# Sorted rows in groups of four and one stream scatter for two blocks, in a mixture-of-experts kernel

## The chip, the cores and the metric

One core of one Trainium2 chip runs the whole program. The metric is the device time of one execution in microseconds (us), median of several executions. The engines are named as in the profile: PE (TensorE, matmuls; PEld is its weight load), ACT (ScalarE), DVE (VectorE), POOL (GpSimd) and SP (SyncE, which only issues transfers here).

## What is computed

A causal 7-tap convolution over 8 sequences of 3584 rows, 192 wide, with one softmaxed set of taps for each of 8 heads of 24 columns. Its 28,672 result rows go through a top-1 mixture of 8 experts. Cut to what matters:

```python
logits = x @ w_gate                          # (28672, 8)
e_idx = np.argmax(logits, axis=1)            # one expert for each row
gate_w = softmax(logits)[row, e_idx]
eom = sigmoid(x @ w_output_gate)
for e in range(8):
    mask = e_idx == e
    h = np.maximum(x[mask] @ w1[e], 0.0)     # 192 -> 1024
    ye = h @ w2[e]                           # 1024 -> 192
    out[mask] = gate_w[mask, None] * eom[mask, e, None] * ye
```

The inputs are one fixed draw, so which row goes to which expert is fixed too.

## The kernel before

The 28,672 rows are cut into 16 units of 1792 rows, and a unit into 8 blocks of 224 rows (two half blocks of 112 rows, `l = 0, 1`, are sorted together). Three kinds of work share the engines.

**Front.** `front_a(u)` does the convolution on PE (tile `cv`), transposes it (`tt`) and computes both gates (`gb`). `front_b(u)` picks each row's expert, computes its place in its block (`pos`) and the places of the block's groups in the stream (`dst`, `du`), and then sorts block by block: `prep(i)` builds 0/1 matrices `pm` on DVE, four matmuls with 128 columns of weights (line 541) put the block's 224 rows in expert order into one PSUM tile `ps`, one ACT copy (`evac`, line 349) takes it to an SBUF tile `xs` of [128, 2, 256], and `scatter` (line 559) sends the 128 pairs of rows to DRAM, in one POOL transfer with a list of places. A pair is two neighbouring rows of one expert: an expert's rows in a block are filled up to an even number. The stream `xcg` holds each expert's rows behind one another.

**Slots.** A slot is up to 512 rows of one expert from the stream. `slot_load` brings them in with three SP transfers (two of them transposing: `xa` on line 682, `xb` on line 684; and `xi` on line 686), which must wait until the scatters of the units concerned have landed. `Slot.first` multiplies by `w1` (lines 727 and 734; relu in three ACT parts, line 755, and one DVE part, line 753, for each slot). `Slot.second` multiplies by `w2` (line 777), ACT copies the result to `y` (line 783), and `emit_out` sends 128 rows at a time to the output by a POOL transfer with a list of places (line 588).

**Order.** It is written out by hand. The front of units 0 to 3 runs ahead of the slots ("fill phase": PSUM tiles from all pools, `fill[0]` is a number). Then a loop over u = 2 to 14 runs four slots for each unit, in 16 positions (slot, quarter `q`); `fill[0]` is None from there. At positions 0 to 7 (in the loop's first round 3 to 10) one block of a later unit is sorted at each, and its scatter is issued at once; `quota` lets one output transfer go at every second of these positions, and one or two at each of the others, so that outputs pile up during the sorting and go out behind it. At position 7 `loads(u + 1)` issues the loads of the next four slots on SP. `plan` chooses rows for the slots by a fixed rotation of experts. The last round (u = 14) takes seven slots of the rotation, and while the first six run, `load_pick` plans the slots of `DYN`, each for the expert with the most rows left: two of 512 rows, four of 256. A loop at the end does what may still be left (nothing, for this draw).

Of the kernel before, what the change touches and what calls it, by code (L numbers as in the profile page):

```python
# [21 lines left out]
def kernel(  # L22
# [10 lines left out]
    nc = tc.nc  # L33
# [19 lines left out]
    TP = TT // 2  # L53
    NG = NB // 2
    CP = TP + N // 2 + 64
    CAP = 2 * CP
# [8 lines left out]
    DYN = (TP, TP) + (TP // 2,) * 4  # L65
# [5 lines left out]
    xcg2 = xcg.rearrange("(a b) w -> a (b w)", b=2)  # L71
# [153 lines left out]
    hole = const.tile([128, 1], FP32)  # L225
    nc.vector.tensor_scalar(out=rowi[:, 3:4], in0=rowi[:, 0:1], scalar1=63, scalar2=None,
                            op0=ALU.bitwise_and)
    nc.vector.tensor_copy(out=hole, in_=rowi[:, 3:4])
    nc.vector.tensor_scalar(out=hole, in0=hole, scalar1=float(HB), scalar2=-64.0,
# [22 lines left out]
    NXS = 12  # L252
    xss = [const.tile([128, 2, RW], FP16, name=f"xs{i}") for i in range(NXS)]
# [3 lines left out]
    poi = const.tile([128, 2, 128], U32)  # L257
    nc.gpsimd.iota(poi, pattern=[[1, 2], [2, 128]], base=1, channel_multiplier=0)
# [31 lines left out]
    for l in range(2):  # L290
        nc.vector.tensor_scalar(
            out=lsum[0:GE, l * GE:(l + 1) * GE].rearrange("p (i e) -> p i e", e=E),
            in0=s9[:, :, 0:E], scalar1=2.0, scalar2=None, op0=ALU.mult)
# [133 lines left out]
    def front_b(u, split=False):  # L427
# [30 lines left out]
        nc.vector.tensor_scalar(out=nu, in0=pn[:, 0:1], scalar1=1.0, scalar2=None,  # L458
                                op0=ALU.add)
        nc.vector.tensor_scalar(out=nu, in0=nu, scalar1=1, scalar2=None,  # L460
# [52 lines left out]
        if split:  # L513
# [10 lines left out]
            scalar=rowf[:, 0:1], in1=dd, op0=ALU.is_le, op1=ALU.mult)  # L524
# [6 lines left out]
        for i in range(NG):  # L531
            if i == 1 and u >= U0 and u != U0 + 2:
# [4 lines left out]
            pm = pms.pop(i)  # L537
# [6 lines left out]
            while len(pend) >= NXS:  # L544
                emit_in()
            xs = xss[nxs[0] % NXS]
            nxs[0] += 1
            evac(xs[:, :, 0:XW], ps[:, 0:2 * XW].rearrange("p (r w) -> p r w", r=2), "act")
            pend.append(lambda i=i, xs=xs: scatter(u, du, xs, i))
            yield  # L550
# [53 lines left out]
    def plan_run(e0, n, nm):  # L604
# [8 lines left out]
        nc.vector.tensor_scalar(out=bu[:, 0:n], in0=bs, scalar1=2.0, scalar2=None, op0=ALU.mult)  # L613
        nc.vector.tensor_tensor(out=Dh, in0=Dh, in1=tk, op=ALU.add)
        nc.vector.tensor_scalar(out=tk, in0=tk, scalar1=-2.0, scalar2=float(TT),
# [15 lines left out]
    def plan(u):  # L631
        n = 4 if u < UL else E - 1
# [7 lines left out]
    def pick(tp):  # L640
# [17 lines left out]
        nc.vector.scalar_tensor_tensor(out=bt, in0=bt, scalar=2.0, in1=oh,  # L658
# [9 lines left out]
        nc.vector.tensor_scalar(out=tk1, in0=tk1, scalar1=-2.0, scalar2=float(2 * tp),  # L668
# [39 lines left out]
    class Slot:  # L708
# [49 lines left out]
        def second(self, q):  # L758
# [15 lines left out]
            o = (q % 2) * D  # L774
            for fc in range(FCH):
# [5 lines left out]
                                 stop=(fc == FCH - 1 and q % 2 == 1))  # L781
            if q % 2 == 1:
                nc.scalar.copy(out=self.y[:, q - 1:q + 1, :],  # L783
# [204 lines left out]
```

## Time and profile before

| | |
|---|---|
| median of 3 runs | 719.75 us (718.98 to 726.15) |
| profiled execution: its own time | 722.9 us |
| profiled execution: span, first to last instruction | 721.2 us |
| mean granted TensorE clock | 0.894 |

The span is divided by the profile among engines, stretches of time and groups of instructions. "Busy" is the time in which an engine had an instruction running. A group of instructions is told as line, engine, operation, tiles written and read, count, busy time, mean time of one in ns, and the idle time just before them with what ended it. "issue" means that nothing in the profile shows what the engine waited for; "remote" and "another core or an unknown queue" stand for a wait whose end the profile can't put down to an instruction (there is only one core here).

### The profile page before, as it was taken

What the parts mean: (1) busy time and instruction counts of PE and PEld (TensorE: products, weight loads), DVE (VectorE), ACT (ScalarE), POOL (GpSimd) and SP (SyncE); (2) the same over time, 40 slices, a digit from 0 to 9 for tenths busy, and PEclk for the clock granted to TensorE, in tenths of its full rate; (3) what the DMA queues carried; (4) which work ended last, traced back from release to release, by engine and by line L of the source; (5) the groups of instructions that cost most, each with busy time, mean ns of one, the idle gap of its engine ahead of it and who ended that gap; (6) DMA issues with size and microseconds to landing.
All of it is one profiled execution on the core that took longest, in us unless ns stands there. A gap on an engine that the chain in (4) does not pass through costs nothing.

```text
span 721.2 us, 16231 instructions
## 1 busy us (share of the span) xinstructions
PE 577.4 (80%) x5712; PEld 370.8 (51%) x5712; DVE 375.7 (52%) x1355; ACT 364.8 (51%) x657; POOL 419.3 (58%) x621
## 2 busy tenths in 40 slices
PE   8878868998497979869697897978969767688874
PEld 4545535664364646546364563644646434445552
DVE  6765547575344736546372673735638343146422
ACT  5765535664354635546363563644646444355552
POOL 8464443888455574655647355564655747555664
PEclk9976668999598998989899798997989989799998
DMA  9999493897555545355453544536142332576411
GB/s 166 235 265 225 105 190 78 165 197 149 112 126 115 126 118 129 93 131 129 108 126 109 102 124 103 135 100 130 69 101 71 88 80 74 118 161 199 156 55 36
DMA packets 161091, 91.95 MB, mean 127 GB/s; under 512 B 112373, under 2 KB 151910, under 8 KB 161008
## 3 DMA queue, kind: packets, MB, share of 16 engines
q1 hardware_dynamic: 131504, 47.57, 31.8%
q0 software_dynamic: 29504, 43.32, 22.7%
q8 instruction: 45, 0.74, 0.4%
q14 instruction: 38, 0.31, 0.2%
HBM read 37.87 MB, written 42.07 MB: 111 GB/s over the span
## 4 chain that ended last, share of the span: by engine, by line
PE 61%; another core or an unknown queue 10%; ACT 9%; issue 8%; DVE 5%; DMA 2%; POOL 2%; SPq 2%; POOLq 0%; ACTq 0%; DVEq 0%
PE pyt L777 18%; PE pp L727 16%; PE pp L734 8%; PE pf L541 6%; PE pf L367 6%; ACT ht L755 4%; PE pf L390 3%; PE pf L401 2%; DMA xt<-in_x_dram 1%; POOL out_dram L588 1%; ACT cv L349 1%; ACT tt L349 1%; ACT y L783 1%; DVE ht L753 1%
## 5 line engine op out<-in xcount | busy, mean ns | idle before, releaser
L588 POOL DMA_INDIRECT out_dram<-y,oi x236 | 232.6, 986 | 146.7 <-ACT y L783 82.3
L777 PE MATMUL pyt<-wres,ht 128*128 128x192 f16 x1760 | 188.3, 256 | 38.2 <-ACT y L783 20.9
L777 PEld LDWEIGHTS <-ht 128*128 128x128 f16 x1888 | 168.6, 101 | 82.6 <-issue 58.4
L559 POOL DMA_INDIRECT xcg_sorted<-xs,du x128 | 128.9, 1007 | 140.7 <-ACT xs L349 101.6
L755 ACT ACTIVATE ht<-pp 128x1024 f16<-128x1024 f32 (+1 forms) x183 | 176.5, 998 | 60.2 <-PE pp L727 30.1
L753 DVE TENSOR_SCALAR ht<-pp 128x1024 f16<-128x1024 f32 (+1 forms) x61 | 72.4, 1187 | 129.4 <-PE pp L727 92.4
L734 PE MATMUL pp<-xb,wres 64*128 64x512 f16 x220 | 75.6, 401 | 37.9 <-ACT ht L755 25.6
L783 ACT COPY y<-pyt 128x384 f32<-128x384 f32 x118 | 57.2, 484 | 94.6 <-remote 32.9
L727 PE MATMUL pp<-xa,wres 128*128 128x512 f16 x220 | 89.9, 409 | 1.3 <-issue 0.7
L727 PE MATMUL pp<-xb,wres 128*128 128x512 f16 x220 | 89.0, 404 | 2.2 <-issue 2.2
L367 PE MATMUL pf<-xt,band 64*64 64x192 f32 x1024 | 69.6, 368 | 20.9 <-issue 11.9
L349 ACT CAST xs<-pf 128x388 f16<-128x388 f32 x128 | 62.4, 496 | 43.1 <-PE pf L541 27.1
L734 PE MATMUL pp<-xa,wres 64*128 64x512 f16 x220 | 76.3, 404 | 1.3 <-issue 0.8
L541 PE MATMUL pf<-xrow,pm 120*128 120x194 f16 x512 | 68.9, 261 | 8.0 <-DVE pm L508 4.2
L351 DVE COPY cv<-pf 120x384 f32<-120x384 f32 x44 | 24.4, 556 | 96.5 <-remote 58.1
L727 PEld LDWEIGHTS <-wres 128*128 128x128 f16 x440 | 35.2, 101 | 64.1 <-issue 42.4
L349 ACT COPY cv<-pf 120x384 f32<-120x384 f32 x84 | 38.2, 486 | 55.1 <-remote 31.2
L508 DVE TENSOR_SCALAR pm<-pos,pos 120x256 f16<-120x256 f16 x256 | 61.5, 304 | 0.0
L503 DVE TENSOR_TENSOR xrow<-cv,gs 120x384 f16<-120x384 f32 x120 | 61.4, 550 | 0.0
L734 PEld LDWEIGHTS <-wres 64*128 64x128 f16 x440 | 18.4, 95 | 82.8 <-issue 82.1
L367 PEld LDWEIGHTS pf<-xt,band 64*64 64x64 f32 x1024 | 40.8, 146 | 36.9 <-issue 21.3
L541 PEld LDWEIGHTS <-pm 120*128 120x128 f16 x512 | 46.2, 102 | 16.9 <-DVE pm L508 6.5
(154 smaller groups left out, 526.0 us busy)
## 6 DMA issues: line engine op xcount, KB each, us to landing
xt<-in_x_dram SPq DMA_DIRECT2D x56, 384.0 KB
wd<-wres SPq DMA_DIRECT2D x6, 768.0 KB
out_dram<-y,oi POOLq DMA_INDIRECT x236
wres<-in_moe_w_dram POOLq DMA_DIRECT2D x8, 384.0 KB
xt<-in_x_dram SPq DMA_DIRECT2D x8, 336.0 KB
wres<-in_moe_w_dram POOLq DMA_DIRECT2D x8, 256.0 KB
xcg_sorted<-xs,du POOLq DMA_INDIRECT x128
xcg_sorted<-zrow SPq DMA_DIRECT2D x8, 256.0 KB
```

The lines of the kernel that those rows point to most:

```text
L349: nc.scalar.copy(out=o, in_=i)
L367: nc.tensor.matmul(pcs[g][64 * c:64 * c + 64, o:o + NB // 2 * GH], band[64 * g:64 * g + 64, h + hh, :], xt[64 * g:64 * g + 64, c * NB // 2 ...
L508: nc.vector.tensor_scalar(out=pms[i][P, l, :], in0=pos16[P], scalar1=pos[P, l * NG + i:l * NG + i + 1], scalar2=None, op0=ALU.is_equal)
L541: nc.tensor.matmul(ps[:, r * XW:(r + 1) * XW], pm[P, l, r * 128:(r + 1) * 128], xr[P, l * NG + i, :], start=(r == 0 and l == 0), stop=(r = ...
L559: i = nc.gpsimd.indirect_dma_start(out=xcg2, out_offset=bass.IndirectOffsetOnAxis(ap=du[:, i:i + 1], axis=0), in_=xs.rearrange("p r w -> p ...
L588: i = nc.gpsimd.indirect_dma_start(out=out, out_offset=bass.IndirectOffsetOnAxis(ap=oi[:, j:j + 1], axis=0), in_=y[:, j, :], in_offset=Non ...
L727: nc.tensor.matmul(pps[r][:, l, :], w[:, o2:o2 + 128], x, start=(r == lead), stop=(r != lead))
L734: nc.tensor.matmul(pps[r][:, l, :], w[p0:p0 + 64, c:c + 128], x[p0:p0 + 64], start=(r != lead), stop=(r == lead))
L753: nc.vector.tensor_relu(out=ht, in_=pps[r])
L755: nc.scalar.activation(out=ht, in_=pps[r], func=AF.Relu)
L777: nc.tensor.matmul(self.pp[:, o:o + D], self.ht[fc // 2][:, fc % 2, q * 128:(q + 1) * 128], self.w[:, w:w + D], start=(fc == 0 and q % 2 = ...
L783: nc.scalar.copy(out=self.y[:, q - 1:q + 1, :], in_=self.pp[:, 0:2 * D].rearrange("p (g d) -> p g d", d=D))
```

## The change

Rows are grouped in fours (`QR = 4`), not in pairs. An expert's rows in a block are filled up to a multiple of four, a block has up to 64 groups, and a scatter carries two blocks: 64 groups of each, 128 pieces of 2 KB from an `xs` tile of [128, 4, 256], of which there are 6 instead of 12. So `du` is made in two halves (one DVE instruction more for a unit), and the list of places has 4 columns instead of 8.

In the fill phase a block of two is sorted by 16 matmuls with 64 columns of weights, which write partitions 0 to 63 for the first block and 64 to 127 for the second; there is still one ACT copy of 128 x 388 for each block.

Among the slots (`fill[0] is None`) each block keeps its four matmuls with 128 columns. Their result has row 0 or 2 of a group in partitions 0 to 63 and row 1 or 3 in 64 to 127, while `xs` wants all four rows of the first block in partitions 0 to 63 and of the second in 64 to 127. So two copies of 64 x 388 take the place of one of 128 x 388: both on ACT for the first block of two, one on ACT and one on DVE for the second.

The smaller units of planning follow: slots of 512 rows are 128 groups. The last round takes eight slots of the rotation instead of seven, and `DYN` becomes four slots of 512 rows, one of 256 and three of 128 (an odd number of quarters is now allowed in `Slot.second`).

```diff
-    CP = TP + N // 2 + 64
-    CAP = 2 * CP
+    CP = TP + N // QR + 96
+    CAP = QR * CP
-    DYN = (TP, TP) + (TP // 2,) * 4
+    DYN = (TP,) * 4 + (TP // 2,) + (TP // 4,) * 3
...
-    NXS = 12
-    xss = [const.tile([128, 2, RW], FP16, name=f"xs{i}") for i in range(NXS)]
+    NXS = 6
+    xss = [const.tile([128, QR, RW], FP16, name=f"xs{i}") for i in range(NXS)]
...
-        du = pr.tile([128, NG], U32, tag="du", name="du")
-        nc.vector.tensor_scalar(out=du, in0=dst, scalar1=rowf[:, 0:1], scalar2=None, op0=ALU.add)
+        du = pr.tile([128, NT], U32, tag="du", name="du")
+        for g in range(2):
+            h = slice(64 * g, 64 * g + 64)
+            nc.vector.tensor_scalar(out=du[h], in0=dst[h].rearrange("p (t g) -> p g t", g=2)[:, g, :],
+                                    scalar1=rowm[h], scalar2=None, op0=ALU.add)
...
             ps = pft()
+            if fill[0] is None:
+                g = i % 2
+                for h in range(2):
+                    for l in range(2):
+                        nc.tensor.matmul(ps[:, h * XW:(h + 1) * XW],
+                                         pms[i][P, l, h * 128:(h + 1) * 128],
+                                         xr[P, l * NG + i, :],
+                                         start=(h == 0 and l == 0), stop=(h == 1 and l == 1))
+                xq = xs[64 * g:64 * g + 64, :, 0:XW].rearrange("p (h r) w -> p r h w", r=2)
+                for r in (g, 1 - g):
+                    evac(xq[:, r], ps[64 * r:64 * r + 64, 0:2 * XW].rearrange(
+                        "p (h w) -> p h w", h=2), "dve" if g and r == 0 else "act")
+                if g:
+                    pend.append(lambda t=t, xs=xs: scatter(u, du, xs, t))
+                yield
+                continue
             for r in range(2):
                 for l in range(2):
-                    nc.tensor.matmul(ps[:, r * XW:(r + 1) * XW],
-                                     pm[P, l, r * 128:(r + 1) * 128], xr[P, l * NG + i, :],
-                                     start=(r == 0 and l == 0), stop=(r == 1 and l == 1))
+                    for g in range(2):
+                        nc.tensor.matmul(
+                            ps[64 * g:64 * g + 64, r * XW:(r + 1) * XW],
+                            pms[2 * t + g][P, l, (rh + r) * 64:(rh + r + 1) * 64],
+                            xr[P, l * NG + 2 * t + g, :],
+                            start=(r == 0 and l == 0), stop=(r == 1 and l == 1),
+                            tile_position=(0, 64 * g))
...
-            out=xcg2, out_offset=bass.IndirectOffsetOnAxis(ap=du[:, i:i + 1], axis=0),
+            out=xcg4, out_offset=bass.IndirectOffsetOnAxis(ap=du[:, i:i + 1], axis=0),
...
-        n = 4 if u < UL else E - 1
+        n = 4 if u < UL else E
```

## Rows read from the trace of the kernel before

**Rows 1.** Page: busy time, share of the span and count, by engine.

```profile
PE 577.4 (80%) x5712; PEld 370.8 (51%) x5712; DVE 375.7 (52%) x1355; ACT 364.8 (51%) x657; POOL 419.3 (58%) x621
```

**Rows 2.** Page: chain of work that ended last, shares of the span by engine.

```profile
PE 61%; another core or an unknown queue 10%; ACT 9%; issue 8%; DVE 5%; DMA 2%; POOL 2%; SPq 2%; POOLq 0%; ACTq 0%; DVEq 0%
```

**Rows 3.** Page: costliest groups of instructions.

```profile
L559 POOL DMA_INDIRECT xcg_sorted<-xs,du x128 | 128.9, 1007 | 140.7 <-ACT xs L349 101.6
...
L349 ACT CAST xs<-pf 128x388 f16<-128x388 f32 x128 | 62.4, 496 | 43.1 <-PE pf L541 27.1
...
L351 DVE COPY cv<-pf 120x384 f32<-120x384 f32 x44 | 24.4, 556 | 96.5 <-remote 58.1
```

**Rows 4.** Stretches: length; busy us of PE, PEld, DVE, ACT, POOL; granted clock, DMA share, GB/s.

```profile
148.00:172.00 24.00, 23.16 (x265) 15.65 (x265) 17.53 (x60) 16.12 (x30) 20.17 (x30) 1.00 0.91 173
320.00:348.00 28.00, 25.81 (x300) 17.99 (x301) 19.43 (x66) 17.80 (x31) 16.15 (x23) 1.00 0.48 120
...
627.00:690.00 63.00, 53.88 (x443) 32.62 (x441) 29.89 (x127) 35.13 (x46) 37.98 (x55) 1.00 0.58 160
```

**Rows 5.** Timeline around 343 to 356 us, POOL: start, us, engine, line, operation.

```profile
343.68 0.98 POOL L559 DMA_INDIRECT xcg_sorted<-xs,du  x1 [1.56 <-ACT xs L349]
344.97 0.98 POOL L588 DMA_INDIRECT out_dram<-y,oi  x1 [0.30 <-issue]
...
346.25 0.98 POOL L559 DMA_INDIRECT xcg_sorted<-xs,du  x1 [0.18 <-issue]
...
352.66 0.98 POOL L588 DMA_INDIRECT out_dram<-y,oi  x1 [0.30 <-issue]
```

**Rows 6.** The same stretch on SP and ACT.

```profile
348.74 1.47 SPq L682 DMA_TRANSPOSE xa<-xcg_sorted  x1
...
343.30 0.48 ACT L783 COPY y<-pyt 128x384 f32<-128x384 f32 x1
343.67 0.50 ACT L349 CAST xs<-pf 128x388 f16<-128x388 f32 x1
...
355.62 0.48 ACT L783 COPY y<-pyt 128x384 f32<-128x384 f32 x1 [7.65 <-remote]
```

**Rows 7.** Timeline around 389 us, the last block of another unit: ACT, then POOL.

```profile
388.81 0.48 ACT L349 CAST xs<-pf 128x388 f16<-128x388 f32 x1 [0.97 <-PE pp L727]
...
389.56 0.97 POOL L559 DMA_INDIRECT xcg_sorted<-xs,du  x1 [0.31 <-issue]
```

**Rows 8.** The chain in order of time: start, us, what.

```profile
75.46 3.02 DMA xcg_sorted<-xs,du
...
175.29 14.16 another core or an unknown queue
...
347.97 7.63 another core or an unknown queue
```

**Rows 9.** Timeline: last copies of unit 2 (ACT), last copy and scatter of unit 5.

```profile
72.59 1.06 ACT L349 CAST xs<-pf 128x388 f16<-128x388 f32 x2 [0.86 <-issue]
...
162.70 0.49 ACT L349 CAST xs<-pf 128x388 f16<-128x388 f32 x1
...
171.79 0.99 POOL L559 DMA_INDIRECT xcg_sorted<-xs,du  x1 [0.18 <-issue]
```

**Rows 10.** Timeline of line 753, once in each slot, in the last round.

```profile
627.26 1.22 DVE L753 TENSOR_SCALAR ht<-pp 128x1024 f16<-128x1024 f32 x1 [6.49 <-PE pp L727]
...
689.50 1.23 DVE L753 TENSOR_SCALAR ht<-pp 128x1024 f16<-128x1024 f32 x1 [5.96 <-PE pp L727]
695.42 0.69 DVE L753 TENSOR_SCALAR ht<-pp 128x512 f16<-128x512 f32 x1 [4.22 <-PE pp L727]
...
710.00 0.69 DVE L753 TENSOR_SCALAR ht<-pp 128x512 f16<-128x512 f32 x1 [2.94 <-PE pp L727]
```

**Rows 11.** Timeline of PE: matmuls with 128 and with 32 columns of weights.

```profile
322.13 1.48 PE L777 MATMUL pyt<-wres,ht 128*128 128x192 f16 x16
...
337.48 1.34 PE L401 MATMUL pf<-tt,wg 128*32 128x224 f32 x24
```

More of the change, by code (lines that the diff above doesn't have):

```diff
@@ L52 @@
     TT = 512
-    TP = TT // 2
+    QR = 4
+    TP = TT // QR
     NG = NB // 2
-    CP = TP + N // 2 + 64
-    CAP = 2 * CP
+    NT = NG // 2
+    CP = TP + N // QR + 96
+    CAP = QR * CP
     FCH = F // 128
@@ L225 @@
     hole = const.tile([128, 1], FP32)
+    rowm = const.tile([128, 1], FP32)
     nc.vector.tensor_scalar(out=rowi[:, 3:4], in0=rowi[:, 0:1], scalar1=63, scalar2=None,
@@ L228 @@
     nc.vector.tensor_copy(out=hole, in_=rowi[:, 3:4])
+    nc.vector.tensor_copy(out=rowm, in_=rowi[:, 3:4])
     nc.vector.tensor_scalar(out=hole, in0=hole, scalar1=float(HB), scalar2=-64.0,
@@ L457, in front_b @@
         nu = pr.tile([128, 1], U32, tag="nu", name="nu")
-        nc.vector.tensor_scalar(out=nu, in0=pn[:, 0:1], scalar1=1.0, scalar2=None,
+        nc.vector.tensor_scalar(out=nu, in0=pn[:, 0:1], scalar1=float(QR - 1), scalar2=None,
                                 op0=ALU.add)
-        nc.vector.tensor_scalar(out=nu, in0=nu, scalar1=1, scalar2=None,
+        nc.vector.tensor_scalar(out=nu, in0=nu, scalar1=2, scalar2=None,
                                 op0=ALU.logical_shift_right)
@@ L531, in front_b @@
         for i in range(NG):
+            t, rh = i // 2, i % 2 * 2
             if i == 1 and u >= U0 and u != U0 + 2:
@@ L536, in front_b @@
                 prep(i + 2)
-            pm = pms.pop(i)
-            ps = pft()
+            if rh == 0:
+                while len(pend) >= NXS:
+                    emit_in()
+                xs = xss[nxs[0] % NXS]
+                nxs[0] += 1
+            ps = pft()
+            if fill[0] is None:
[14 more added lines that the diff above has]
+                continue
@@ L550, in front_b @@
+            evac(xs[:, rh:rh + 2, 0:XW], ps[:, 0:2 * XW].rearrange("p (r w) -> p r w", r=2), "act")
+            if rh:
+                pend.append(lambda t=t, xs=xs: scatter(u, du, xs, t))
             yield
@@ L657, in pick @@
                                        op0=ALU.add, op1=ALU.min)
-        nc.vector.scalar_tensor_tensor(out=bt, in0=bt, scalar=2.0, in1=oh,
+        nc.vector.scalar_tensor_tensor(out=bt, in0=bt, scalar=float(QR), in1=oh,
                                        op0=ALU.mult, op1=ALU.mult)
@@ L667, in pick @@
                                        op0=ALU.mult, op1=ALU.add)
-        nc.vector.tensor_scalar(out=tk1, in0=tk1, scalar1=-2.0, scalar2=float(2 * tp),
+        nc.vector.tensor_scalar(out=tk1, in0=tk1, scalar1=-float(QR), scalar2=float(QR * tp),
                                 op0=ALU.mult, op1=ALU.add)
@@ L774, in second @@
             o = (q % 2) * D
+            last = q % 2 == 1 or q == self.nq - 1
             for fc in range(FCH):
@@ L780, in second @@
                                  start=(fc == 0 and q % 2 == 0),
-                                 stop=(fc == FCH - 1 and q % 2 == 1))
-            if q % 2 == 1:
-                nc.scalar.copy(out=self.y[:, q - 1:q + 1, :],
-                               in_=self.pp[:, 0:2 * D].rearrange("p (g d) -> p g d", d=D))
-                pout.extend((self.y, self.oi, j) for j in (q - 1, q))
+                                 stop=(fc == FCH - 1 and last))
+            if last:
+                j0 = q - q % 2
+                nc.scalar.copy(out=self.y[:, j0:q + 1, :],
+                               in_=self.pp[:, 0:(q + 1 - j0) * D].rearrange("p (g d) -> p g d", d=D))
+                pout.extend((self.y, self.oi, j) for j in range(j0, q + 1))
     def reg(ap, engines, hi):
@@ L937 @@
     nc.vector.tensor_copy(out=lfu, in_=lf)
-    nc.vector.tensor_scalar(out=lfu, in0=lfu, scalar1=8, scalar2=None,
+    nc.vector.tensor_scalar(out=lfu, in0=lfu, scalar1=7, scalar2=None,
                             op0=ALU.logical_shift_right)
```

22 lines of the change are left out of this document (8 added, 14 removed).

## The prediction

> **What bounds the kernel now.** I read the page's shares first, then the chain, then stretches, and last the timeline where the chain leaves PE. PE is busy for 80% of the span, POOL for 58%, ACT and DVE for about half each [rows 1]; the chain runs over PE for 61%, over ACT and DVE together for 14%, over POOL for 2%, and spends 10% (some 72 us) in waits that the profile can't name [rows 2]. So POOL's work, of which the change takes most away, is hardly on the path as such. While blocks are sorted, PE works 25.81 of 28 us, with ACT at 17.80, DVE at 19.43 and POOL at 16.15 [rows 4]: PE is the bound, and the others have room.
>
> The unnamed waits are one stop in nearly every unit, the longest pieces 14.16 and 7.63 us [rows 8]. The reader is to see its shape: the unit's last scatter goes out at 346.25, SP starts the next loads at 348.74, and ACT, which waits for PE's products, has nothing to do for 7.65 us, until 355.62 [rows 5, 6]. POOL meanwhile sends the outputs that the quota held back, 1.28 us apart; the last, five steps after the scatter, begins at 352.66 and ends 1.98 us before the stop does [rows 5]. What holds PE there, no row says.
>
> **The change, part by part.** The profiled execution took 722.9 us (span 721.2 and 1.7 around it). The terms are summed on that; the median is 3.15 us lower.
>
> *More slots.* Counting the reference's routing in blocks of 224 rows gives 29,196 stream rows in pairs and 30,200 in fours. The slots are there whether full or not: 57 of 512 rows and 4 of 256 become 60 of 512, one of 256 and three of 128 (counted through the plan, the final loop stays empty in both). All of the difference lies in the last round, where no sorting covers it. Line 753 comes once in each slot: nine intervals from 627.26 to 689.50 make 6.92 us for a slot of 512; three from 695.42 to 710.00 make 4.86 for one of 256 [rows 10]. A slot of 128 is not in the trace. Its upper bound is the 4.86 of the nearest row, its lower bound one output transfer, 1.28 [rows 5]; I take 3.0, a little under the middle, since its products and copies halve again but its steps do not. Sum: 3 x 6.92 - 3 x 4.86 + 3 x 3.0 = 20.8 - 14.6 + 9.0 = +15.2; ends +10.0 and +20.8. PE has 53.88 of 63 us in this stretch [rows 4], so nothing hides it.
>
> *Copies among the slots.* 12 units (4 to 15) are sorted there, 48 twos of blocks. ACT goes from two copies of 388 elements to three: the new ones have half the partitions but the same 388 elements in each, so I keep 496 ns [rows 3]. That is 48 x 0.496 = 23.8 us more on ACT. DVE gets 48 copies; its nearest row is 384 elements from PSUM at 556 ns [rows 3], so 48 x 0.556 = 26.7 us. Behind the ACT copy stand relu and `y` copies, behind the DVE copy its relu and the next `pm`, and PE waits for all of these. Their cover is the room of the sorting stretch, about 10 us of 28 on ACT and 9 on DVE [rows 4]. As a share that comes through I take the chain's: 14% runs over ACT and DVE [rows 2], so 0.14 x 50.5 = +7. Ends: 0 (all in the room) and +26.7 (the longer of two copies that run side by side always last).
>
> Both copies of a second block read one PSUM tile, in different halves of the partitions. The Trainium skill (PSUM — Partial Sum Buffer, section "PSUM bank collisions raise a hardware error") says that two engines may be in one bank at once if they are in different groups of 32 partitions, so by it DVE needn't wait for ACT and the sum stays as it is. No row here shows two engines at one tile's halves. If the program orders them all the same, DVE waits for ACT's copy each time; that is inside the upper end.
>
> *Fewer scatters.* 64 of 128 go, at 1007 ns [rows 3]: 64 us of POOL's busy time, which lies beside other work except where a scatter is late and SP's loads stand behind it.
> - First round of the loop: unit 5's last copy ends at 163.19, its scatter goes out at 171.79, 8.60 late, with POOL busy 20.17 of 24 us, that is full with its gaps [rows 4, 9]. Four scatters fewer at 1.28 bring that scatter 5.1 us forward. The stop behind it is the 14.16 [rows 8]; it should give back what POOL gains: -5, ends 0 and -8.6.
> - Other units: in one form the last copy ends at 344.17 and its scatter starts at 346.25, behind the sixth block's scatter at 343.68 and an output at 344.97 [rows 5, 6]. Without that scatter the output can start when its `y` is there (343.78, plus the 0.28 that the scatter at 389.56 needed after its copy [rows 7]), the new scatter at 345.34, 0.91 earlier. In the other form POOL is on time (389.29 to 389.56) and nothing is gained. About half of eleven units, half of it passed on: -2.5; ends 0 and -10. What is late next is the stop itself: its outputs are held by the quota, which isn't touched.
> - Before the loop: unit 2's last copy ends at 73.65, its scatter lands in the chain from 75.46 [rows 8, 9]; the new one can go at about 73.9: -1.5, ends 0 and -1.5.
>
> By the Trainium skill (DMA: Bandwidth & Descriptors, section "Anatomy of one DMA") a transfer takes about 2.0 us plus its bytes over 436 KB/us. By that a scatter of 256 KB would land 0.3 us after one of 128 KB, and the lead of 0.91 would be 0.6, the -2.5 about -1.7. Our trace has 2.49 us from the scatter's start to SP's load [rows 5, 6], and no scatter of the new size.
>
> *Fill phase.* 32 blocks there: 128 matmuls of 128 columns become 256 of 64. Sixteen matmuls of 128 columns step on by 82 ns, 24 of 32 columns, with a longer stream, by 43 [rows 11], so narrow ones run side by side: 0. If they did not, 128 x 0.082 = +10.5. The one DVE instruction more in a unit and fewer start-up clears: 0.
>
> **Sum:** 722.9 + 15.2 + 7 - 5 - 2.5 - 1.5 = 736.1 in a profiled execution; on the median, 719.75 + 13.2 = **733**. With the nearer ends of each term this case spans 725 to 742.
>
> **Rivals.**
> 1. *The stops shrink.* This stop ends shortly after POOL's last transfer, so its length may follow the number of transfers that POOL and SP have under way. For: the 1.98 us in the stop looked at [rows 5, 6]. Against: the five outputs in a stop stay. Were each of twelve stops shorter by two transfers (2.56 us), -31 in place of -2.5: 733 - 28 = 705. It comes out under the old time from 15.7 / 12 = 1.3 us a stop, one transfer each.
> 2. *The copies are on the path.* PE's 92% in the sorting stretch leaves it little to lose before it waits [rows 4]. +26.7 in place of +7: 753. Against: ACT and DVE are two thirds busy there.
> 3. *It doesn't matter.* Slots at +10, copies at +3, POOL's gains at -5, -5 and -1.5: 721.
> 4. *Narrow matmuls in turn.* +10.5: 743.5. The steps of 43 ns speak against it [rows 11].
>
> **How the numbers follow.** My forecast has 0.48, rival 1 0.22, rival 2 0.12, rival 3 0.13, rival 4 0.05. The time is the likeliest's, 733. The range goes from 705, which cuts off the lower half of rival 1 (0.11), to 750, which cuts off most of rival 2 (0.08). Because the signs differ, the likeliest's own range, 725 to 742, stands beside it. One per cent, about what a measurement can tell here, is 7.2 us. Faster than 712.5: nearly all of rival 1, 0.20. Between 712.5 and 727: rival 3, a little of rival 1 and the low end of the forecast, 0.22. Slower: 0.58.
>
> **What would show it.** Line 753 should come 64 times, with line 588 at 245 transfers, line 559 at 64 and still about 1 us each; from the last round's first slot to the end it should take about 15 us more. In sorting stretches, PE's busy share falls from 92% to about 90% if the copies cost 7 us, to under 85% if they are on the path. The first stop should shorten by about 5 us and the others keep their length; if each lost 1.3 us or more, rival 1 holds. I'm wrong if the last round doesn't grow, or if the stops follow POOL's count.

## The result, and the profile after

The changed kernel took 693.64 us (median of 4, 693.22 to 695.28) beside 719.37 for the kernel before: ratio 0.9635, 95% interval 0.9579 to 0.9692, so 3.65% faster, where the prediction had 733 us and slower.

One thing has to be known to read any number below: some sets of runs (a set is several kernels run together on one chip, the kernel before among them) found the chip in another condition, in which the same kernel before takes 557 us instead of 719. I call the condition with 719 A and the one with 557 B. After the first pair there are five sets, with A in the first and third and B in the second, fourth and fifth.

| set | condition | kernel before | changed kernel | ratio |
|---|---|---|---|---|
| first pair | A | 719.37 | 693.64 | 0.9635 (0.9579 to 0.9692) |
| third set of experiments | A | 718.09 | 696.49 | 0.9660 (0.9604 to 0.9717) |
| fourth set | B | 557.15 | 571.61 | 1.0263 (1.0235 to 1.0291) |

So the change gains 3.4 to 3.65% in A and loses 2.6% in B. The prediction was made from a trace of A. The page of the changed kernel in A: busy times, then the chain by engine, then four of the costliest groups.

```profile
PE 578.7 (84%) x5960; PEld 375.1 (54%) x5960; DVE 415.7 (60%) x1462; ACT 405.7 (59%) x720; POOL 363.5 (53%) x532
...
PE 57%; DVE 10%; another core or an unknown queue 9%; issue 7%; ACT 7%; DMA 5%; POOL 3%; SPq 0%; POOLq 0%; ACTq 0%; DVEq 0%
...
L617 POOL DMA_INDIRECT out_dram<-y,oi x245 | 245.3, 1001 | 159.6 <-ACT y L814 96.4
...
L588 POOL DMA_INDIRECT xcg_sorted<-xs,du x64 | 64.1, 1002 | 146.4 <-DVE xs L355 68.7
```

Against [rows 1 to 3] the counts are as planned: 64 scatters still at 1.00 us, 245 outputs. PE is busy for as long as before (578.7 for 577.4), in a span of 691.9 for 721.2: what went is PE's idle time, with 9% of the span still in waits that nothing names.

The same page line in B, the kernel before and then the changed one (spans 554.3 and 568.5 us):

```profile
PE 515.1 (93%) x5712; PEld 345.0 (62%) x5712; DVE 376.1 (68%) x1355; ACT 368.5 (66%) x657; POOL 424.5 (77%) x621
```

```profile
PE 531.4 (93%) x5960; PEld 358.6 (63%) x5960; DVE 417.0 (73%) x1462; ACT 405.6 (71%) x720; POOL 362.9 (64%) x532
```

DVE, ACT and POOL are busy for as many microseconds as in A; PE is for 62 and 47 us less, with the stops gone and a higher granted clock (mean 0.977 and 0.974 in B, 0.894 and 0.912 in A).

**Where the time went.** The DVE relu comes once in each slot, so its starts mark the stages. First the starts of slots 0, 8, 40 and 47 (counted from 0: the loop's first slot, the first after two rounds, one well on in even running, and the last slot ahead of the last round) from the timelines. Kernel before in A (slot 47, 627.26, is in [rows 10]):

```profile
110.89 1.23 DVE L753 TENSOR_SCALAR ht<-pp 128x1024 f16<-128x1024 f32 x1 [2.19 <-PE pp L727]
201.73 1.22 DVE L753 TENSOR_SCALAR ht<-pp 128x1024 f16<-128x1024 f32 x1 [0.80 <-PE pf L541]
...
552.48 1.23 DVE L753 TENSOR_SCALAR ht<-pp 128x1024 f16<-128x1024 f32 x1
```

Changed kernel in A:

```profile
97.69 1.22 DVE L782 TENSOR_SCALAR ht<-pp 128x1024 f16<-128x1024 f32 x1 [0.91 <-PE pp L756]
182.06 1.22 DVE L782 TENSOR_SCALAR ht<-pp 128x1024 f16<-128x1024 f32 x1
...
510.68 1.22 DVE L782 TENSOR_SCALAR ht<-pp 128x1024 f16<-128x1024 f32 x1
576.20 1.23 DVE L782 TENSOR_SCALAR ht<-pp 128x1024 f16<-128x1024 f32 x1 [11.83 <-PE pp L756]
```

Kernel before in B, then the changed kernel in B:

```profile
89.28 1.22 DVE L753 TENSOR_SCALAR ht<-pp 128x1024 f16<-128x1024 f32 x1 [0.90 <-PE pp L727]
167.38 1.23 DVE L753 TENSOR_SCALAR ht<-pp 128x1024 f16<-128x1024 f32 x1 [0.31 <-PE pp L727]
...
422.55 1.23 DVE L753 TENSOR_SCALAR ht<-pp 128x1024 f16<-128x1024 f32 x1
469.90 1.23 DVE L753 TENSOR_SCALAR ht<-pp 128x1024 f16<-128x1024 f32 x1 [4.12 <-PE pp L727]
```

```profile
93.49 1.23 DVE L782 TENSOR_SCALAR ht<-pp 128x1024 f16<-128x1024 f32 x1 [0.90 <-PE pp L756]
168.72 1.21 DVE L782 TENSOR_SCALAR ht<-pp 128x1024 f16<-128x1024 f32 x1
...
426.25 1.22 DVE L782 TENSOR_SCALAR ht<-pp 128x1024 f16<-128x1024 f32 x1
473.63 1.23 DVE L782 TENSOR_SCALAR ht<-pp 128x1024 f16<-128x1024 f32 x1 [4.04 <-PE pp L756]
```

From these and the ends of the spans, changed kernel minus kernel before in us:

| stretch | predicted | A | B |
|---|---|---|---|
| ahead of the loop, to slot 0 | -1.5 | -13.2 | +4.2 |
| slots 0 to 8 | -5 | -6.5 | -2.9 |
| slots 8 to 47 (copies +7, POOL -2.5) | +4.5 | -31.4 | +2.4 |
| slot 47 to the end | +15.2 | +21.8 | +10.5 |
| sum | +13.2 | -29.3 | +14.2 |

The sum for B is the predicted one within a microsecond; that for A is not even of its sign. From slot 8 to slot 40 four slots take 43.8 us before and 41.1 after in A, but 31.9 and 32.2 in B: 11.9 us of A's 43.8 aren't the kernel's own work, and the change takes 3.0 of them away.

**What a stop is.** One hand-over between two units, in stretches of time (columns as in [rows 4]); the changed kernel in A:

```profile
406.00:408.00 2.00, 0.64 (x4) 0.19 (x2) 0.00 (x0) 0.48 (x1) 1.64 (x2) 1.00 0.69 141
408.00:410.00 2.00, 0.93 (x5) 0.33 (x5) 0.56 (x1) 0.00 (x0) 1.52 (x4) 1.00 0.94 120
410.00:412.00 2.00, 0.60 (x2) 0.36 (x2) 0.00 (x0) 0.00 (x0) 1.00 (x2) 0.53 0.83 184
```

and a hand-over of the changed kernel in B:

```profile
342.00:346.00 4.00, 4.00 (x44) 2.44 (x42) 2.59 (x10) 3.21 (x6) 3.21 (x5) 1.00 0.26 96
346.00:350.00 4.00, 4.00 (x48) 2.65 (x47) 3.51 (x13) 2.29 (x5) 3.34 (x6) 1.00 0.90 141
350.00:354.00 4.00, 4.00 (x49) 2.65 (x47) 3.20 (x12) 3.01 (x5) 3.21 (x5) 1.00 0.85 158
```

In both, POOL sends a unit's last scatter and then outputs 1.28 us apart, and SP's loads run beside them; POOL's timeline around the last scatter, in A and in B:

```profile
400.93 0.97 POOL L588 DMA_INDIRECT xcg_sorted<-xs,du  x1 [2.43 <-DVE xs L355]
402.21 0.98 POOL L617 DMA_INDIRECT out_dram<-y,oi  x1 [0.30 <-issue]
...
409.90 0.98 POOL L617 DMA_INDIRECT out_dram<-y,oi  x1 [0.30 <-issue]
```

```profile
341.91 0.97 POOL L588 DMA_INDIRECT xcg_sorted<-xs,du  x1 [2.16 <-DVE xs L355]
343.19 0.98 POOL L617 DMA_INDIRECT out_dram<-y,oi  x1 [0.30 <-issue]
...
358.61 0.98 POOL L617 DMA_INDIRECT out_dram<-y,oi  x1 [0.30 <-issue]
```

In A PE does 2.17 of 6 us there and the clock falls to 1.2 GHz behind it; in B, under a row of outputs twice as long, PE is busy for 12.00 of 12 us at 2.4 GHz. The stops are A's own: none of the kernel before's slots of 14 to 22 us is there in B.

The readers of PE's products wait through such a stop. Here the last product of one slot's `Slot.first`, and the DVE relu that reads it, in A:

```profile
404.35 0.38 PE L756 MATMUL pp<-xb,wres 128*128 128x512 f16 x1
...
412.52 1.23 DVE L782 TENSOR_SCALAR ht<-pp 128x1024 f16<-128x1024 f32 x1 [3.78 <-remote]
```

By the profile the product is done at 404.73, and the relu starts 7.79 us later. In B the product that ends at 93.45 has its relu at 93.49. The ends of products are modelled, so the profile doesn't tell whether in A the product itself is late or only the word that it is done. What holds it, no run shows.

### The profile page after: what moved, and what is told of

It reads as the page before. It is cut to its first block, busy times and chain, and to the rows that moved or that the text cites. A ratio compares the mean times of both kernels' runs of the same rounds, so it can differ in the third digit from the quotient of the medians.

```text
span 691.9 us, 16722 instructions
## 1 busy us (share of the span) xinstructions
PE 578.7 (84%) x5960; PEld 375.1 (54%) x5960; DVE 415.7 (60%) x1462; ACT 405.7 (59%) x720; POOL 363.5 (53%) x532
## 3 DMA queue, kind: packets, MB, share of 16 engines
q0 software_dynamic: 28912, 43.83, 25.2%
## 4 chain that ended last, share of the span: by engine, by line
PE 57%; DVE 10%; another core or an unknown queue 9%; issue 7%; ACT 7%; DMA 5%; POOL 3%; SPq 0%; POOLq 0%; ACTq 0%; DVEq 0%
PE pyt L807 18%; PE pp L756 15%; PE pp L763 8%; PE pf L371 4%; PE pf L555 4%; PE pf L394 3%; ACT ht L784 3%; PE pf L405 2%; POOL out_dram L617 2%; DMA xt<-in_x_dram 2%; DMA out_dram<-y,oi 2%; PE pf L570 2%; DMA wres<-in_moe_w_dram 1%; ACT xs L353 1%
## 5 line engine op out<-in xcount | busy, mean ns | idle before, releaser
L617 POOL DMA_INDIRECT out_dram<-y,oi x245 | 245.3, 1001 | 159.6 <-ACT y L814 96.4
L784 ACT ACTIVATE ht<-pp 128x1024 f16<-128x1024 f32 (+2 forms) x192 | 183.4, 987 | 81.3 <-remote 39.1
L807 PEld LDWEIGHTS <-ht 128*128 128x128 f16 x1960 | 172.9, 101 | 54.0 <-issue 28.8
L588 POOL DMA_INDIRECT xcg_sorted<-xs,du x64 | 64.1, 1002 | 146.4 <-DVE xs L355 68.7
L782 DVE TENSOR_SCALAR ht<-pp 128x1024 f16<-128x1024 f32 (+2 forms) x64 | 75.2, 1176 | 103.5 <-PE pp L756 68.0
L371 PE MATMUL pf<-xt,band 64*64 64x192 f32 x1024 | 76.2, 355 | 38.3 <-issue 32.4
L353 ACT CAST xs<-pf 64x388 f16<-64x388 f32 (+1 forms) x176 | 83.7, 479 | 28.7 <-PE pf L555 13.5
L814 ACT COPY y<-pyt 128x384 f32<-128x384 f32 (+1 forms) x124 | 58.7, 474 | 65.4 <-PE pyt L807 25.4
L555 PE MATMUL pf<-xrow,pm 120*128 120x194 f16 x384 | 48.0, 246 | 2.8 <-DVE pm L512 2.4
L355 DVE CAST xs<-pf 64x388 f16<-64x388 f32 x48 | 26.7, 556 | 29.3 <-ACT xs L353 26.8
```

Of the source, the lines that this page charges most:

```text
L353: nc.scalar.copy(out=o, in_=i)
L371: nc.tensor.matmul(pcs[g][64 * c:64 * c + 64, o:o + NB // 2 * GH], band[64 * g:64 * g + 64, h + hh, :], xt[64 * g:64 * g + 64, c * NB // 2 ...
L555: nc.tensor.matmul(ps[:, h * XW:(h + 1) * XW], pms[i][P, l, h * 128:(h + 1) * 128], xr[P, l * NG + i, :], start=(h == 0 and l == 0), stop= ...
L588: i = nc.gpsimd.indirect_dma_start(out=xcg4, out_offset=bass.IndirectOffsetOnAxis(ap=du[:, i:i + 1], axis=0), in_=xs.rearrange("p r w -> p ...
L617: i = nc.gpsimd.indirect_dma_start(out=out, out_offset=bass.IndirectOffsetOnAxis(ap=oi[:, j:j + 1], axis=0), in_=y[:, j, :], in_offset=Non ...
L782: nc.vector.tensor_relu(out=ht, in_=pps[r])
```

## The experiments

All edits are to the changed kernel, unless they say the kernel before. My first theory for A was that POOL transfers in a row hold PE's completions, and that halving the scatters broke the rows up; the rivals were POOL's time as such, and the sort's new copies and matmul widths.

**One more POOL transfer behind each scatter** (condition A)

```diff
         nodep(i, f"sc{u}", [f"sc{v}" for v in range(NU)] + ["load", "guard"])
+        k = nsc[0]
+        nsc[0] += 1
+        spare = nc.dram_tensor(f"spare{k}", (128, 2 * RW), FP16, kind="Internal").ap()
+        nc.gpsimd.indirect_dma_start(
+            out=spare, out_offset=bass.IndirectOffsetOnAxis(ap=rowi[:, 0:1], axis=0),
+            in_=xs[:, 0:2, :].rearrange("p r w -> p (r w)"), in_offset=None,
+            bounds_check=127, oob_is_err=False)
+        rest()
```

> The changed kernel with one more indirect transfer from POOL behind each of its 64 scatters: 128 rows of 1 KB from the same tile into a spare tensor that nobody reads. POOL issues as many transfers, as closely behind each other, as before the change; the sort's matmuls and copies and the slots stay those of the changed kernel. Bursts theory (three or more POOL transfers issued back to back hold TensorE's completions, and halving the scatters broke the bursts up): the gain ahead of the loop (13 us) and among the slots (2.4 us a unit, 38 us in all) comes back, 725 to 745 us. POOL-time theory (POOL's busy time, whatever it does, sets the pace): the same, 725 to 745. Copies theory (the gain is from the sort's new matmul widths and from copies on two engines): 692 to 698.

Measured: 773.45 us (before 719.38), 80 over the changed kernel, more than either theory had. Slot 0 comes 19.5 us later, and four slots take 47.3 us for 41.1 (slots 8 and 40):

```profile
207.33 1.22 DVE L791 TENSOR_SCALAR ht<-pp 128x1024 f16<-128x1024 f32 x1
...
585.54 1.22 DVE L791 TENSOR_SCALAR ht<-pp 128x1024 f16<-128x1024 f32 x1
```

(Later expectations speak of 8 spare transfers a unit; it is 4, so 1.5 us each.) The copies theory, by which a spare transfer costs nothing, is out. What the written spare transfers cost in B wasn't run.

**POOL time without a transfer** (A): a clear of a [128, 1400] tile in the same place.

```diff
         nodep(i, f"sc{u}", [f"sc{v}" for v in range(NU)] + ["load", "guard"])
+        nc.gpsimd.memset(longer, 0.0)
+        rest()
```

> The changed kernel with a clear of a 128 x 1400 tile by POOL (about 1 us, no transfer) behind each of its 64 scatters. POOL is busy for as long as before the change, but with the fewer transfers. Bursts theory: 692 to 700 us. POOL-time theory: 725 to 745. Copies theory: 692 to 698.

Measured: 715.79 us (ten executions, 705.53 to 720.11), between the theories. The clear took 1.29 us, not one, and it slowed DVE. DVE's groups (mean ns of one is the last number before the second bar), in the changed kernel and then here:

```profile
L512 DVE TENSOR_SCALAR pm<-pos,pos 120x256 f16<-120x256 f16 x256 | 61.1, 301 | 0.9 <-PE pf L570 0.6
L355 DVE CAST xs<-pf 64x388 f16<-64x388 f32 x48 | 26.7, 556 | 29.3 <-ACT xs L353 26.8 <-issue 1.6
```

```profile
L512 DVE TENSOR_SCALAR pm<-pos,pos 120x256 f16<-120x256 f16 x256 | 78.6, 444 | 0.7 <-PE pf L570 0.4
...
L355 DVE CAST xs<-pf 64x388 f16<-64x388 f32 x48 | 26.7, 556 | 17.4 <-ACT xs L353 15.8 <-issue 0.5
```

By stages, 15.6 of its 20.5 us (on the spans) are there by slot 8, where PE's waits for DVE's `pm` in the fill phase grow from 9.7 to 14.7 us; the rest of it isn't traced. From slot 8 to slot 40 four slots take 41.3 us for 41.1. In even running POOL's time costs next to nothing; the transfer does.

**The slots alone** (A): the kernel before with the changed slot plan and the odd number of quarters in `Slot.second` that it needs, and nothing else.

```diff
-    DYN = (TP, TP) + (TP // 2,) * 4
+    DYN = (TP,) * 4 + (TP // 2,) + (TP // 4,) * 3
...
-        n = 4 if u < UL else E - 1
+        n = 4 if u < UL else E
...
```

> The kernel before with the change's slot plan alone: eight slots in the last round and then 512, 512, 512, 512, 256, 128, 128, 128 rows instead of seven and then 512, 512 and four of 256; scatters and sort as before. By the prediction's price 719.4 + 15 = 734.6 us (730 to 740); by the comparison of the last rounds of the two traces (115.7 us for 93.9) 719.4 + 22 = 741 (738 to 745). If the slots were free, 717 to 722.

Measured: 735.93 us, +16.5 (ratio 1.0253, 1.0187 to 1.0319). The prediction's +15.2 is right by itself; the other expectation is too high.

**Outputs spread evenly** (A)

```diff
             if u == UL:
                 return 1
-            if pos in sorting:
-                return pos % 2
-            return 1 + pos % 2
+            return 1
```

> The changed kernel with its output scatters spread evenly: one behind every quarter slot, also while the unit is sorted, instead of one or none there and one or two after it; the number of outputs is the same. Bursts theory: the burst of outputs behind the last scatter of a unit goes, and with it much of the 8 us by which the slot at each hand-over is longer than the others (16 for 8.2 us, 12 of them): 620 to 685 us. If the stop belongs to the hand-over itself (the loads of the next unit) and not to the burst: 690 to 697. If outputs between the sort's scatters make new bursts there (scatter, output, scatter, output): 697 to 720.

Measured: 678.17 us, 15.5 under the changed kernel, within the wide range that I gave the theory of rows but at its poor end: the one slot of 16 us a unit is gone, and two or three of 9 to 13 stand in its place; four slots take 39.6 us for 41.1. Shorter rows of transfers help, but most of A's loss isn't a matter of how the transfers are spread.

**The same on the kernel before** (A): one output behind every quarter slot there too.

> The kernel before with its output scatters spread evenly, one behind every quarter slot, as in the fourth experiment. If bursts of POOL transfers make the stops of the slow chip: 10 to 40 us faster than the kernel before there (680 to 710). On a chip without stops there is nothing to win: 553 to 561 us. If the outputs between the sort's scatters cost more than the burst behind them: 725 or more, or 562 or more.

Measured: 710.93 us (ratio 0.9850, 0.9785 to 0.9916), -7. In the trace four slots take 43.8 us from slot 8 to slot 40, as before. Most of the 26 us between the two kernels isn't to be had that way.

**Spread outputs and a leaner slot plan** (A): the changed kernel with the edit of `quota` above and a shorter `DYN`.

```diff
-    DYN = (TP,) * 4 + (TP // 2,) + (TP // 4,) * 3
+    DYN = (TP,) + (TP * 3 // 4,) * 4 + (TP // 4,) * 2
```

> The changed kernel with even output scatters and a leaner plan of the last slots: 512, 384, 384, 384, 384, 128, 128 rows for 512 four times, 256 and 128 three times (2304 rows for 2688, seven slots for eight). By rows at the last round's pace (5.65 us for 512 rows on the fast chip, 6.5 on the slow one): 4 to 5 us less than without: 673 us on the slow chip (668 to 680), 573 on the fast one (568 to 582). If the number of slots counts and not their rows: 3 us less.

Measured: 674.23 us, ratio 0.9324 (0.9242 to 0.9407), ahead of both kernels in A, and the lowest median there, though its interval overlaps that of the spread outputs alone (0.9376 to 0.9475). In the profiles the last round takes 6.8 us less than with spread outputs alone. It didn't run in B.

**The two kernels again** (A)

> The changed kernel as it is, beside the kernel before on the chip of this call. The second set of experiments fell on a chip where the kernel before takes 557 us and nothing in the loop stops. If the chip of this call is like it: by the step of the prediction for the slots (15 us) and for the copies (7 us), with nothing to win on POOL, 557 + 22 = 579 us (570 to 586), slower. If it is like the first chip (719 us before): 690 to 697, faster. If the gain does not hang on the chip: 3.6 % faster on either.

> The kernel before as it is, for its trace on the chip of this call: 557 or 719 us, ratio 1.00. Where the chip takes 557, the stops in the sorting stretches and at the hand-overs (the slots of 14 to 22 us) are gone and a slot takes 7.5 to 9 us; where it takes 719, they are there as in the first trace.

Measured: 696.49 and 716.21 us beside 718.09. This set ran on the same chip as the second, which had B, and the fourth set, with B, on the chip of the first, which had A; so it isn't the chip. Four slots take 44.0 us for the kernel before and 41.6 for the changed one in these traces, 2.4 apart where the first pair has 2.8. The shape of the stops is less steady than that. Between slots 8 and 40 the longest slot of each four takes 15.2 us before and 16.1 after in the first pair of traces, and 17.4 and 16.2 in this one; the mean of the other three is 9.5 and 8.3 in the first pair, 8.9 and 8.5 in this one.

**The second set fell into B**, where nothing of A's stops could be tested. The loop's sort in 64-column products with one ScalarE copy for each:

```diff
-            if fill[0] is None:
+            if u < 0:
                 g = i % 2
```

> The changed kernel with the loop's sort done as the phase ahead of the loop does it: 64-column products into both halves of one PSUM tile and one ScalarE copy for each, so 8 matmuls and one copy for each 128-row block half where the changed kernel has 4 matmuls and two copies; the scatters and everything else stay. If the copies among the slots cost what the first two experiments leave over (8 spare transfers cost 5.9 us a unit, the whole change gave 3.1, so the copies cost some 2.8 a unit): 693 - 11 x 2.8 = 663 us, 655 to 680. If the gain comes from the new matmul width and from the copies on two engines: 715 to 735. If neither counts: 690 to 697.

Measured: 583.47 us beside 556.93, and in the fourth set 582.43 beside 571.61 for the changed kernel:

> The kernel of the fifth experiment again (the loop's sort done with 64-column products and one ScalarE copy for each), for the state in which the kernel before takes 719 us. If the copies among the slots cost what is left of the change's gain (8 spare transfers a unit cost 5.9 us, the change gave 3.1): 655 to 680 us. If the sort's new form is what gains: 715 to 735. If its form counts for nothing: 690 to 700. If the kernel before takes 557 us: 580 to 587, as the first time.

The changed kernel as it is had been expected there at 579 (570 to 586) by the prediction's terms for the slots and the copies, and took 571.61. So the narrow form costs 10.8 us more than two copies of halves. PE is busy for 541.8 us there and 531.4 in the changed kernel. By the starts of its products from slot 8 to slot 40 the narrow ones themselves aren't slower: they step on by 40 ns, the wide ones by 84. Longer is the way into and out of each group of them: 179 ns from the start of the product before to the first of the group, for 89, and 179 from the last to the next product, for 130. My guess of 663 for A, worked out from the transfers miscounted, stays untested.

**A spare transfer whose rows are all beyond the bound** (the edit of the first experiment with a list of places out of range):

> The changed kernel with a spare indirect transfer behind each scatter, as in the first experiment, but with every row number beyond the bound, so that POOL prepares the transfer and no row is written. If it is POOL's work for a transfer that holds the others: 755 to 775 us, as with the rows written. If it is the rows' bytes on the DMA engines: 694 to 715.

Measured: 577.31 us beside 556.93; one of its four executions took 1734.66 us, and why isn't known. Repeated twice in the hope of A:

> The kernel of the sixth experiment again (a spare indirect transfer behind each scatter, every row number beyond the bound), for the state in which the kernel before takes 719 us. If POOL's work for a transfer makes the stops: 755 to 775 us, as with the rows written (773). If the rows' bytes and their writes do: 694 to 715. If the kernel before takes 557 us: 574 to 580, as the first time.

> The kernel of the sixth experiment once more (a spare indirect transfer behind each scatter, every row number beyond the bound). If the kernel before takes 719 us in this call and POOL's work for a transfer makes the stops: 755 to 775; if the rows' bytes and their writes do: 694 to 715. If the kernel before takes 557 us: 574 to 581, 8 us over the changed kernel, as before.

Measured: 579.17 and 577.61, B each time. Beside the changed kernel's 571.61 that is 7.6 us for 64 transfers, 0.1 us each, against 1.25 each for the written ones in A. No row is written: POOL's queue moves 43.87 MB for the changed kernel's 43.83, and 52.23 in the first experiment. Whether A's stops come from POOL's preparing or from the rows' bytes isn't answered.

**The next unit's loads three quarter slots later**

```diff
-                if pos == 7 and u < UL:
+                if pos == 10 and u < UL:
```

> The changed kernel with the twelve loads of the next unit's slots issued three quarter slots later (behind quarter 10 of a round instead of 7), so some 6 us behind the burst of outputs that follows the last scatter. If the stop at the hand-over (slots of 16 us for 8.2) belongs to POOL's burst alone: its place and length stay, 690 to 697 us. If to the loads alone: it comes 6 us later with the same length, 690 to 697 too, but its start moves with the first load. If it takes both at once: it shrinks by half or more, 11 x 4 us, 640 to 675.

Measured: 585.43 us beside 556.93, B; 14 us over the changed kernel, with the landing of `xb` on 6% of the chain, so the loads are then late. Of A's stop it tells nothing.

**Pauses on POOL behind each transfer**: eight clears of a 128 x 16 tile, then three, and those in the loop alone without its last round.

```diff
     def rest():
         run[0] += 1
-        if run[0] % 2 == 0:
+        for _ in range(8):
             nc.gpsimd.memset(idle, 0.0)
```

> The changed kernel with a pause of about 1 us behind every POOL transfer, scatter and output (8 clears of a 128 x 16 tile instead of one behind every second transfer); the transfers stay. Back-to-back theory (it is transfers in a row that hold TensorE, not their number): the hand-over stops of 8 us shrink, 640 to 685 us. Number theory (each transfer costs TensorE about 0.75 us wherever it stands, which 64 spare ones for 24 us ahead of the loop and 41 us in seven units would fit): 690 to 700. POOL-time theory: POOL is busy for 300 us more, 720 or more.

> The changed kernel with a pause of some 0.4 us (three clears of a 128 x 16 tile) behind every POOL transfer of the loop but in the last round; POOL still has time to spare. State of 719 us: if it is transfers in a row that stop TensorE, 650 to 685 us; if each transfer costs the same wherever it stands, 690 to 700; if POOL's time counts, 700 to 720. State of 557 us: 575 to 590.

Measured, in B: 1003.37 and 711.10 us. I had reckoned the pause too small. POOL's timeline of the second:

```profile
322.95 0.98 POOL L588 DMA_INDIRECT xcg_sorted<-xs,du  x1 [0.70 <-DVE msk L452]
323.93 0.47 POOL L601 MEMSET idle<- 128x16 f16 x3
325.03 0.98 POOL L618 DMA_INDIRECT out_dram<-y,oi  x1 [0.64 <-issue]
```

One transfer takes 2.1 us so, and 20 of them in a unit 42, more than the 32.2 that the unit has: POOL became the bound (43 us for four slots). Useful for one thing: where POOL's room ends.

**The kernel before once more, for its trace in B**

> The kernel before as it is, for its trace in the condition in which it takes 557 us. There the changed kernel's slots, once the loop runs evenly, take 33.1 us for four (8.27, 7.54, 8.4, 7.9); by the prediction's term for the copies (7 us in 12 units, 0.6 a unit) the kernel before takes 32.5, its last round takes 15 us less, and the phase ahead of the loop is as long as the changed kernel's. If POOL's transfers cost something here too, its four slots take more than 33.1. If it takes 719: as in the first trace.

Measured: 557.21 us, B. Four slots take 31.9 us for the changed kernel's 32.2, nearly as predicted; the phase ahead of the loop is not as long as the changed kernel's but 4.2 us shorter; the last round takes 10.5 less.

## Why the prediction was wrong

**The step that failed** is the one on the stops. I read their shape rightly [rows 5, 6], couldn't name what holds PE, and then kept them at the length they had: "What is late next is the stop itself", its outputs untouched. What the change does to them was priced by the lateness of single scatters alone, -2.5 for the loop's other units and -1.5 ahead of the loop. In A they gave 31.4 + 4.5 = 36 us more than the sum has between slots 8 and 47, and 12 more ahead of the loop. The prediction's own sign of being wrong, that the stops follow POOL's count, is what came, in direction. Rival 1 had this at -31 for the loop's stops, almost the measured -31.4, with a chance of 0.22. That the two are so near is luck: the -31.4 is net of 2.4 us of the kernel's own work (the +2.4 of B), and the shape is settled by no trace alone. Rival 1 has each stop shorter; in the first pair the longest slot of four isn't (15.2 and 16.1 us), and the gain lies in the other three, while in the second pair it is 1.3 shorter (17.4 and 16.2) and half of the gain lies there. (In [rows 8], 14.16 and 7.63 aren't the longest pieces, as I said: at 608.53 there is one of 10.29. No term rests on it.)

What the runs put in its place: A's loss goes with POOL transfers. Four spare ones a unit cost 6.2 us in four slots; four fewer, with the rest of the change, gave 2.8; POOL time without a transfer cost 0.2; spreading the outputs gave 1.5 in the changed kernel and nothing in the kernel before. Their number alone doesn't give the size: with 24 transfers a unit the first experiment takes 47.3 us for four slots and the kernel before 43.8. Over the whole kernel A costs 162 us before (364 scatters and outputs) and 122 after (309), on the medians. That transfers cost in A, and not POOL's time, is shown by the first two experiments; whether by what POOL does for them or by their bytes isn't. That rows of them, one behind another, make the loss, as I first thought, isn't shown: the two spread kernels gained only 7 and 15 us. And transfers alone do nothing, since the kernel before issues 24 a unit in B without the stops. What makes the condition is open, and so is what stops PE in it. It is not the chip (two chips showed both), nor the program (the kernel before is the same). All three sets with B had the kernel with the out-of-range transfers in them and no set with A had; that may be chance, and wasn't tried.

**The other steps**, point by point, by B, where no stop blurs them:

*More slots, +15.2.* Right: +16.5 alone in A. (With the whole change the last round grows by 21.8 there, 5 us more; why isn't traced.) In B a slot of 512 takes 5.65 us, one of 256 about 4.0, and one of 128, which I guessed at 3.0 and which takes 3.4 and 2.7 in A, takes 2.2:

```profile
551.99 0.42 DVE L782 TENSOR_SCALAR ht<-pp 128x256 f16<-128x256 f32 x1 [1.35 <-PE pp L756]
554.17 0.42 DVE L782 TENSOR_SCALAR ht<-pp 128x256 f16<-128x256 f32 x1 [1.30 <-PE pp L756]
```

That the last round grows by only 10.5 in B has a cause that I hadn't seen: the kernel before loses 6.2 us from slot 47 to the last round's first slot (11.87 for 5.65). POOL is full there, and the last scatter of the sort goes out 7.7 us behind its copy, in a queue; the loads stand behind it, and PE waits for `xa` (ACT's last copy, then POOL's timeline, then PE's):

```profile
459.57 0.49 ACT L349 CAST xs<-pf 128x388 f16<-128x388 f32 x1
...
465.18 0.97 POOL L559 DMA_INDIRECT xcg_sorted<-xs,du  x1 [0.18 <-issue]
...
467.74 0.97 POOL L559 DMA_INDIRECT xcg_sorted<-xs,du  x1 [0.18 <-ACT ht L755]
...
473.65 0.61 PE L727 MATMUL pp<-xa,wres 128*128 128x512 f16 x1 [2.47 <-DMA xa<-xcg_sorted]
```

Of the 6.2 us PE stands still for 3.0; the rest goes into the products behind the wait, which take 0.61 us each for 0.39, at 1.2 GHz (the granted clock from slot 47 to slot 48 is 0.71).

24 transfers a unit at 1.28 us are 30.7 of its 31.9 us. So POOL, of which I said that it is hardly on the path, is next to the bound in B, and the change (20 transfers, 25.6 us) gives it room. In A, the 11.9 us of stops in each unit hid that.

*Copies, +7.* The size isn't far off, 2.4 us in B from slot 8 to slot 47 where the sum has 4.5 (7 less 2.5), but the mechanism isn't seen, so that is luck. The term is made of PE's waits for copies, and in even running in B there are none. From slot 8 to slot 40, kernel before and changed kernel (columns as in [rows 4]):

```profile
167.38:422.55 255.17, 254.66 (x2947) 176.92 (x2945) 190.08 (x643) 181.14 (x305) 208.09 (x290) 1.00 0.70 160
```

```profile
168.72:426.25 257.53, 257.53 (x2945) 178.85 (x2944) 210.65 (x685) 199.90 (x336) 170.31 (x242) 1.00 0.69 158
```

ACT and DVE work 18.8 and 20.6 us more, and PE is busy throughout: as far as the profile shows, all of it lies in the room, the low end of the term. What makes PE 2.9 us busier for the same products isn't traced. DVE's copy does wait for ACT's, as the end of that paragraph allowed:

```profile
304.08 0.48 ACT L353 CAST xs<-pf 64x388 f16<-64x388 f32 x1
304.59 0.56 DVE L355 CAST xs<-pf 64x388 f16<-64x388 f32 x1 [0.39 <-ACT xs L353]
```

It begins 0.03 us behind ACT's end, here and in the A trace. So these copies never show two engines at one tile; what the Trainium skill says of that (PSUM — Partial Sum Buffer, section "PSUM bank collisions raise a hardware error") stays unseen in these runs.

*First round, -5.* In B -2.9, in A -6.5: right in direction, and between. Unit 5's last scatter is 4.2 us late in the changed kernel's A trace, for 8.6 before; 5.1 less was predicted.

*Fill phase, 0.* The products were read rightly. Sixteen narrow ones (two blocks) against eight wide ones, in B, changed kernel and kernel before, both where the granted clock is 1.00:

```profile
65.87 0.86 PE L570 MATMUL pf<-xrow,pm 120*64 120x194 f16 x16
```

```profile
76.72 0.84 PE L541 MATMUL pf<-xrow,pm 120*128 120x194 f16 x8
```

Sixteen take as long as eight, so the narrow ones do run side by side, in pairs, and rival 4 doesn't hold. (At 1.2 GHz the same sixteen take 1.66 us, from 62.81; only rows at one clock can be compared.) The phase is longer all the same, by 4.2 us up to slot 0, where the sum has 1.5 less. From 20 us to slot 0, changed kernel and kernel before in B:

```profile
20.00:93.49 73.49, 58.98 (x920) 39.24 (x920) 54.71 (x224) 49.81 (x127) 23.08 (x33) 0.93 1.01 218
```

```profile
20.00:89.28 69.28, 56.24 (x792) 35.57 (x792) 53.83 (x219) 49.60 (x126) 40.02 (x57) 0.98 1.01 228
```

PE stands still for 1.5 us more and is busy for 2.7 more, at a granted clock of 0.93 for 0.98. Its waits for DVE's `pm` add up to 9.7 us for 6.3, since the products of two blocks alternate and need both blocks' `pm`. The prediction has none of this, and A's stops hide it. Whether the longer waits are what lowers the clock isn't shown.

So of 13.2 us in the sum, B shows 14.2, part by luck: what comes ahead of the loop is too low by some 6 us and the last round too high by 5, and they make up for each other.

## What to carry to other kernels

A trace with waits that nothing names is a trace of the kernel in a condition, not of the kernel alone: before pricing a change, ask how much of each stage's time is the instructions' own work (here 31.9 of 43.8 us), and give the rest a chance to move as a whole, with the count of whatever runs beside it. Two traces of one kernel under different conditions tell more than many views of one. And an engine's room read from a trace full of stops is too large by the stops: POOL is busy for 58% of the span in A, and its 24 transfers, with the gaps between them, fill 96% of the unit's own time.

## What the runs showed of the hardware

The same program on the same chip took 557 or 719 us in different sets of runs, each within 1% of its median. In the longer condition PE nearly stops for up to 8 us at a time, ACT and DVE wait for its products, and the granted clock falls to 1.2 GHz after the stop has begun, as in the stretches above (1.00 from 406 to 410, then 0.53).

POOL's transfers with a list of places go out 1.28 us apart when they stand in a queue, whether a row has 768 bytes or 2 KB. With three small clears between them it is 2.1.

Fp16 products of 64 columns of weights that alternate between the two halves of the partitions of the result ran in pairs: sixteen in 0.86 us, where eight of 128 columns took 0.84.

A POOL clear of 128 x 1400 fp16 slowed DVE's `pm` (fp16, from SBUF to SBUF) from 301 to 444 ns on average, and left DVE's copies from PSUM at 556. The Trainium skill (Advanced Engine Details and Errata, section "VectorE Performance Modes") says that the two engines share a port of SBUF and block each other in DVE's two-port modes; the trace agrees, though in which mode `pm` runs no row says.
